# Attention, gated convolution and routed experts on one core: raw key projections, a conversion spread over three engines, a mixed order of the last key tiles, six gather buffers and late probabilities

## The chip, the cores and the metric

The kernel runs on one core of a Trainium2 chip. The metric is the device time in microseconds. Three runs of the kernel before gave 601.50, 601.49 and 603.31 us, a median of 601.5.

## The reference

Three stages are fused. What is computed, cut to its core:

```python
# 1. linear attention; q, k, v are (4, 8, 576, 64), w_phi is (64, 128)
proj = einsum('bhsd,df->bhsf', x, w_phi)
proj = proj - max(abs(proj), axis=-1)
phi  = concat([exp(proj), exp(-proj)])            # 256 features
kv, z = phi(k)^T v, sum_s phi(k)                  # per batch and head
x = phi(q) kv / (phi(q) z + 1e-6)                 # (4, 576, 512)
# 2. gated causal convolution, 5 taps per channel
gate = sigmoid(sum_k conv_w[k] * x[s - 4 + k])
y = (gate * (x @ w_val)) @ w_out
# 3. routing and experts, 8 experts, hidden size 1024
logits = y @ w_gate
e = argmax(logits) at s == 0 or where sigmoid(y @ w_local) < 0.5, else the token's before
p = exp(logits - max); p /= sum(p) + 1e-9
out = p[e] * (relu(y @ w1[e]) @ w2[e])
```

All arrays are float32; w_val, conv_w and w_out are handed to the chip as float64 words.

## The kernel before, in words

The 4 x 576 tokens are 18 tiles of 128. Most products run in a faster single-pass format (fp32r): an operand is split into a high part (a cast on ScalarE, `hi_of`, L48) and a low part (the difference, `lo_of`, L51), and three products take the place of one float32 product: high by high, high by low, low by high.

**Keys, about 4 to 91 us.** For each tile a DMA brings `raw`, `split` (L104) makes `qkh` on ScalarE and `qkl` on GpSimd, and `proj` (L114) multiplies it by `w_phi`, which stands twice on a block diagonal, so that one product serves two heads. A call of `proj` makes half a tile (four heads): two head pairs by three products. Only key tile 0 skips the split: it multiplies `raw` by `wraw` in float32, one product for each head pair (L123). VectorE takes the maximum `m` (L131) and subtracts it, `pp` (L133); ScalarE forms both exponentials `ex`; TensorE adds `kv` (L158). Between these, VectorE converts w_val, w_out and conv_w from float64 words (`from64`, L299 to L323): eight chunks of 128 x 512, six VectorE steps each, of which L319 masks an exponent, L320 and L321 scale and add; four of the chunks' low parts per matrix are GpSimd's.

**Queries and mixing, about 90 to 282 us.** Query tiles are projected in the same way; `tq` (L181) transposes, `nm` (L188) divides, `tx` (L207) transposes x. `conv` (L250) runs taps on VectorE, ScalarE and GpSimd for pairs of tiles. The products of `val` (L379) and `ymm` (L522, the output rows `yps`) are filled in between by a budget in `run` (L602).

**Routing, about 282 to 319 us.** A chain of small steps on VectorE and TensorE builds the tables of gather and scatter columns, `gidx` and `sidx`. The rest of the `yps` products are put between the steps: `yfill(10)` ahead of the first transpose `tp1` (L676, L677), then 5, 5, 5, 5, 3 and all that remain. Then 30 products into `idle` (L757 to L759) use TensorE until the first rows have been gathered. They read `ohl`, whose buffer is let go afterwards.

**Experts, about 319 to 590 us.** Ten static units: eight experts of two row tiles and two overflow units of three row tiles. For each unit, GpSimd gathers the rows `xg` from `y_d` (L812, three buffers, L811), `rows` (L816) transposes and splits them and reads the probabilities `p` (L828 to L835) on VectorE, `unit` (L839) does the first layer `hp` (L850), the activations `hh` on ScalarE and `hlo` on VectorE (L852, L853), the second layer `op` (L862) and the scatter `out` (L868). The next unit's gather is issued as a unit starts (L899); its `rows` are called in `mid` after the unit's first output tile (L911). `between` converts the next unit's weights, `w1h`, `w2h` on ScalarE and `w1l`, `w2l` on VectorE.

The program's order on each engine is the scheduler's: it places the instructions by a model of their times within what data and buffers allow, except where `pin` (L410) keeps an order or `issue_after` holds one instruction behind another. Each engine then works strictly in its order.

Of the kernel before, what the change touches and what calls it, by code (L numbers as in the profile page):

```python
# [30 lines left out]
YLAG = 4  # L31
WARM = 30
FRESH = -1.5 * 2.0 ** -23


@with_exitstack
def body(ctx, tc, qT, kT, v1, wbd, w_val, conv_w, w_out, w_gl, w1, w2, out):
# [66 lines left out]
    def split(nm, t):  # L104

        if t >= NT or (nm, t) in hl_t or (nm, t) == ("k", 0):
            return
        hi = ap.tile([128, 4, 128], F32R, tag="qkh", name="qkh", bufs=2)
        lo = ap.tile([128, 4, 128], F32R, tag="qkl", name="qkl", bufs=2)
        hi_of(A, hi, raw_t[nm, t])  # L110
        lo_of(G, lo, raw_t[nm, t], hi)
        hl_t[nm, t] = (hi, lo)

    def proj(nm, t, hh):  # L114
        raw = raw_t[nm, t]
        if nm == "k" and hh == 1:
            pj = ps_b.tile([128, 4, 128], F32, tag="b", name="pj")
        else:
            pj = ps_p.tile([128, 4, 128], F32, tag="pj", name="pj")
# [55 lines left out]
    def xcols(g):  # L175
        return [(off, n, s == 0, off + 4 * (i + 1)) for i, (off, n, b, s) in enumerate(segments(g * 256, 256))]

    def pq(t, hh):
        pq_t[t, hh] = proj("q", t, hh)

    def tq(t, hh):  # L181
        pp = pq_t.pop((t, hh))
        tp = ps_a.tile([128, 4, 128], F32, tag="a", name="tp")
        for h in range(4):
            PE.transpose(tp[:, h, :], pp[:, h, :], ident)  # L185
        qp_t[t, hh] = both_exp(tp)

    def nm(t, hh):  # L188
        qp = qp_t.pop((t, hh))
        if hh == 0:  # L190
            x_t[t] = ap.tile([128, H, DH], F32, tag="x", name="x", bufs=2)
        ps = ps_a.tile([128, 4, VW], F32, tag="a", name="num")
        for h in range(4):
# [105 lines left out]
    def from64(raw, n, tag):  # L299
# [11 lines left out]

        def first():
            V.tensor_scalar(f, hi, 0x07ffffff, 3, op0=ALU.bitwise_and, op1=ALU.logical_shift_left)
            A.activation(af, hi.bitcast(F32), AF.Abs)

        return f, [
            first,
            lambda: V.scalar_tensor_tensor(b, hi, -0x40000000, f, ALU.bitwise_and, ALU.bitwise_or),
            lambda: V.tensor_scalar(m, b, -0x800000, None, op0=ALU.bitwise_and),  # L319
            lambda: V.scalar_tensor_tensor(mf, top, 0.5, mf, ALU.add, ALU.mult),  # L320
            lambda: V.scalar_tensor_tensor(ff, mf, 2.0 ** -36, bf, ALU.mult, ALU.add),  # L321
            lambda: V.scalar_tensor_tensor(ff, af, 2.0 ** -15, ff, ALU.is_ge, ALU.mult),
        ]  # L323

# [252 lines left out]

    order = []
    for kind in ("k", "q"):
        order += [(kind, t) for t in range(NT)]  # L580
    items = [(kind, t, hh) for kind, t in order for hh in range(2)]
# [60 lines left out]
    route_consts()  # L642
    run(lambda i: (0, 0) if i < 0 else ((i + 1) * 13 // 10 - i * 13 // 10, 0) if i < 36 else (5, 2), lambda i: 2.2 if i > 38 else 0)
    attx.close()
# [30 lines left out]
    tp = pst([NT, 128], "tp1")  # L675
    yfill(10)  # L676
    pin(PE.transpose(tp, rc["code"], ident))  # L677
# [130 lines left out]
    def gather(gcols):  # L808
        xs = []
        for gc in gcols:  # L810
            xg = fx.tile([128, YW], F32, tag="xg", name="xg", bufs=3)  # L811
            G.indirect_dma_start(out=xg, out_offset=None, in_=y_d, in_offset=bass.IndirectOffsetOnAxis(ap=gc, axis=0))  # L812
            xs.append(xg)
        return xs

    def rows(xs, probs):  # L816
# [4 lines left out]
        for j, xg in enumerate(xs):  # L821
# [5 lines left out]
            lo_of(V, xl[:, :, sl], xp, xh[:, :, sl])  # L827
            p = fx.tile([128, 1], F32, tag="p", name="p", bufs=6)  # L828
            if isinstance(probs, int):
                V.tensor_copy(p, xg[:, D + probs:D + probs + 1])  # L830
            else:
                es = fx.tile([128, E], F32, tag="es", name="es")
                V.tensor_scalar(es, io8, probs, None, op0=ALU.is_equal)
                V.tensor_tensor(es, es, xg[:, D:YW], ALU.mult)
                V.tensor_reduce(p, es, axis=AX.X, op=ALU.add)  # L835
            pv.append(p)
        return xh, xl, pv

    def unit(hl, x, scols, between, mid):  # L839
# [5 lines left out]
        for f in range(8):  # L845
# [6 lines left out]
            A.activation(hh[:, f, 0:n], hp[:, 0:n], AF.Relu)  # L852
            V.scalar_tensor_tensor(hlo[:, f, 0:n], hp[:, 0:n], 0.0, hh[:, f, 0:n].bitcast(F32), ALU.max, ALU.subtract)  # L853
            if f % 2 == 1:
                between()
        for j in range(len(pv)):
            op = ps_f.tile([128, 512], F32, tag="op", name="op", bufs=2)
# [33 lines left out]
    xs = gather(cols(gidx, units[0][0], units[0][1]))  # L891
    cur_x = rows(xs, unit_probs(0))
    for i, (c0, n, e) in enumerate(units):
        last = i + 1 == len(units)
        nxt = {}
        work = []
        if not last:
            nxt["w"], pieces = unit_weights(i + 1)
            nxt["xs"] = gather(cols(gidx, units[i + 1][0], units[i + 1][1]))  # L899
            started = [p() for p in pieces[:3]]  # L900
            todo = pieces[3:]
# [7 lines left out]
        def mid():  # L909
            if not last:  # L910
                nxt["x"] = rows(nxt["xs"], unit_probs(i + 1))  # L911

# [49 lines left out]
```

## Time and profile before

| what | value |
|---|---|
| median of three runs | 601.5 us |
| profiled execution | 600.88 us, its span 599.2 us |
| TensorE (PE) | 565.9 us busy, 94% of the span |
| VectorE (DVE) | 373.3 us, 62% |
| ScalarE (ACT) | 314.3 us, 52% |
| GpSimd (POOL) | 231.4 us, 39% |

The profile is of one execution, which took 600.88 us: 1.7 us of it lie outside the span. Line numbers are those of the kernel before. "PEld" is the weight load of TensorE, which overlaps its products. In rows of instructions, a group in square brackets is the time that the engine stood idle before it, and what ended that. The matmul records overlap by design, so a product's price in a full stretch is the distance between starts, not the length of a record.

### The profile page before, as it was taken

Reading aid. Unit: us, or ns where it says so; the run is one execution under the profiler, and the core shown is the slowest. Engines: PE = TensorE matmul, PEld = TensorE weight load, DVE = VectorE, ACT = ScalarE, POOL = GpSimd, SP = SyncE. Lnnn points to the kernel's source line nnn. Section 1 sums busy time; section 2 is a strip of 40 time slices with the busy share of each in tenths; the row PEclk is TensorE's granted clock in tenths of the full one; section 3 lists DMA queues with packets and bytes.
Section 4 is the critical chain, followed back from the end, with each engine's and each line's share of the span. In section 5 each row is a group of like instructions: output and inputs, shape, how many; then the busy total and the mean of one; then the engine's idle time right before and its main releaser. Section 6 shows DMA issues by size and latency. Waiting matters only on the chain. (4 is left out here: it accounts for less than half of the span.)

```text
span 599.2 us, 13671 instructions
## 1 busy us (share of the span) xinstructions
PE 565.9 (94%) x5545; PEld 497.4 (83%) x5546; DVE 373.3 (62%) x744; ACT 314.3 (52%) x581; POOL 231.4 (39%) x257
## 2 busy tenths in 40 slices
PE   7997998999999999998998999999998989999993
PEld 6886987889888988886775888988987879898982
DVE  6999859688877877478504766666554746460110
ACT  5767855665766655555215565564553646441210
POOL 4454323489878876472204102302302123011001
PEclk9999999999999999999998999999999999999997
DMA  8933422101110001034226877866866648520000
GB/s 278 339 101 124 131 74 59 49 2 37 36 38 2 21 19 38 19 124 139 111 107 200 288 237 254 268 181 189 284 186 203 203 137 276 179 90 35 18 18 35
DMA packets 46017, 76.82 MB, mean 128 GB/s; under 512 B 3839, under 2 KB 22399, under 8 KB 45952
## 3 DMA queue, kind: packets, MB, share of 16 engines
q1 hardware_dynamic: 39840, 60.55, 32.5%
q0 software_dynamic: 3520, 10.58, 4.9%
q10 hardware_dynamic: 2592, 4.79, 2.1%
q8 instruction: 45, 0.74, 0.5%
q14 instruction: 20, 0.16, 0.1%
HBM read 66.39 MB, written 10.56 MB: 128 GB/s over the span
## 5 line engine op out<-in xcount | busy, mean ns | idle before, releaser
L868 POOL DMA_INDIRECT out<-osb,sidx x22 | 28.6, 1302 | 206.7 <-ACT osb L867 161.4
L850 PE MATMUL hp<-xh,w1h 128*128 128x256 f32 (+1 forms) x320 | 94.6, 296 | 7.3 <-DVE hlo L853 5.8
L850 PE MATMUL hp<-xh,w1l 128*128 128x256 f32 (+1 forms) x320 | 94.2, 294 | 0.0
L850 PE MATMUL hp<-xl,w1h 128*128 128x256 f32 (+1 forms) x320 | 93.8, 294 | 0.0
L850 PEld LDWEIGHTS hp<-xh,w1h 128*128 128x128 f32 x320 | 60.8, 190 | 10.4 <-DVE hlo L853 7.1
L862 PE MATMUL op<-w2h,hh 128*128 128x512 f32 x176 | 69.1, 401 | 0.2 <-ACT hh L852 0.2
L51 DVE TENSOR_TENSOR w2l<-wraw,w2h 128x1024 fp32r<-128x1024 f32 x40 | 48.9, 1224 | 32.1 <-ACT w2h L48 22.4
L51 POOL TENSOR_TENSOR qkl<-raw,qkh 128x512 fp32r<-128x512 f32 x35 | 46.7, 1334 | 55.5 <-ACT qkh L48 55.4
L862 PE MATMUL op<-w2l,hh 128*128 128x512 f32 x176 | 67.9, 395 | 0.0
L862 PE MATMUL op<-w2h,hlo 128*128 128x512 f32 x176 | 66.8, 395 | 0.0
L51 DVE TENSOR_TENSOR w1l<-wraw,w1h 128x1024 fp32r<-128x1024 f32 x40 | 48.9, 1250 | 22.6 <-ACT w1h L48 22.6
L131 DVE TENSOR_REDUCE m<-pj 128x4 f32<-128x512 f32 x72 | 49.1, 685 | 22.0 <-PE pj L128 21.9
L265 DVE SCALAR_TENSOR_TENSOR acc<-xT,tfs,acc 128x256 f32<-128x256 f32 (+1 forms) x112 | 53.9, 486 | 13.3 <-ACT acc L263 12.0
L850 PEld LDWEIGHTS hp<-xh,w1l 128*128 128x128 f32 x320 | 60.7, 190 | 1.5
L850 PEld LDWEIGHTS hp<-xl,w1h 128*128 128x128 f32 x320 | 60.5, 189 | 0.0
L48 ACT CAST w2h<-wraw 128x1024 fp32r<-128x1024 f32 x40 | 41.8, 1049 | 34.0 <-DMA wraw<-w 25.2
L853 DVE SCALAR_TENSOR_TENSOR hlo<-hp,hh 128x256 fp32r<-128x256 f32 (+1 forms) x80 | 33.9, 445 | 39.6 <-ACT hh L852 39.5
L852 ACT ACTIVATE hh<-hp 128x256 fp32r<-128x256 f32 (+1 forms) x80 | 31.2, 404 | 48.0 <-PE hp L850 47.6
L48 ACT CAST w1h<-wraw 128x1024 fp32r<-128x1024 f32 x40 | 40.4, 1052 | 29.6 <-DMA wraw<-w 29.6
L133 DVE TENSOR_TENSOR pp<-pj,m 128x512 f32<-128x512 f32 x72 | 48.8, 683 | 2.5 <-PE tp L185 0.8
L158 PE MATMUL kv<-v,ex 128*64 128x65 f32 (+1 forms) x1280 | 46.9, 224 | 3.3 <-DVE kvsb L170 1.4
L158 PEld LDWEIGHTS kv<-v,ex 128*64 128x64 f32 (+1 forms) x1280 | 41.0, 137 | 9.3 <-DVE kvsb L170 1.7
(192 smaller groups left out, 1364.5 us busy)
## 6 DMA issues: line engine op xcount, KB each, us to landing
wraw<-w SPq DMA_DIRECT2D x80, 512.0 KB, 4.5
v<-v SPq DMA_DIRECT2D x18, 260.0 KB, 3.2
y_d<-ysb ACTq DMA_DIRECT2D x18, 260.0 KB, 2.0
raw<-qT SPq DMA_DIRECT2D x18, 256.0 KB, 3.4
raw<-kT SPq DMA_DIRECT2D x17, 256.0 KB, 5.0
wr<-w_val SPq DMA_DIRECT2D x4, 512.0 KB, 7.4
wr<-w_out SPq DMA_DIRECT2D x4, 512.0 KB, 7.6
xg<-y_d,gidx POOLq DMA_INDIRECT x22, 5.4
```

Source lines behind the costliest of these rows:

```text
L48: (A.copy if eng is A else eng.tensor_copy)(hi, src)
L51: eng.tensor_tensor(lo, src, hi.bitcast(F32), ALU.subtract)
L131: V.tensor_reduce(m, pj, axis=AX.X, op=ALU.max, apply_absolute_value=True)
L133: V.tensor_tensor(pp, pj, m.unsqueeze(2).to_broadcast([128, 4, 128]), ALU.subtract)
L158: PE.matmul(kv_ps[b][blk // 7][mh * 64:mh * 64 + 64, (blk % 7) * VW:(blk % 7 + 1) * VW], lhsT=kp_t[t, hh][off:off + n, sg, h, mh * 64:mh * ...
L265: W["tap"] = V.scalar_tensor_tensor(acc[c], xs, cw[:, kk, c:c + 1], acc[c], ALU.mult, ALU.add)
L850: PE.matmul(hp[:, 0:n], lhsT=wt[:, k, f * 128:(f + 1) * 128], rhs=xt[:, k, 0:n], start=(i == 0), stop=(i == 11))
L852: A.activation(hh[:, f, 0:n], hp[:, 0:n], AF.Relu)
L853: V.scalar_tensor_tensor(hlo[:, f, 0:n], hp[:, 0:n], 0.0, hh[:, f, 0:n].bitcast(F32), ALU.max, ALU.subtract)
L862: PE.matmul(op, lhsT=ht[:, f, sl], rhs=wt[:, f, :], start=(i == 0), stop=(i == 23))
L868: G.indirect_dma_start(out=out, out_offset=bass.IndirectOffsetOnAxis(ap=scols[j], axis=0), in_=osb, in_offset=None, bounds_check=T - 1, oo ...
```

## The change

`split` returns for every key tile, so all 18 key tiles are projected in float32 from `raw`. `from64` has four steps instead of six: VectorE keeps L313, L318, L319 and L322, ScalarE makes the scaled top word, and GpSimd does the product and the sum. The last three key tiles (MIX = 3) alternate with the first three query tiles; query tiles 0 to 3 take their two PSUM tiles from `ps_b`. `yfill(10)` is `yfill(18)`. The gathers have six buffers (XG = 6), the rows of unit 1 are gathered right behind those of unit 0, and those of unit i + 2 in `mid` of unit i. The probabilities are computed in `unit`, issued behind the last `hlo` of that unit.

```diff
     def split(nm, t):
-        if t >= NT or (nm, t) in hl_t or (nm, t) == ("k", 0):
+        if t >= NT or (nm, t) in hl_t or nm == "k":
             return
...
-        if nm == "k" and hh == 1:
+        if nm == "k" and hh == 1 and t < NT - MIX:
             pj = ps_b.tile([128, 4, 128], F32, tag="b", name="pj")
...
+    def early(t):
+        return ps_b if t <= MIX else ps_a
...
-        tp = ps_a.tile([128, 4, 128], F32, tag="a", name="tp")
+        tp = early(t).tile([128, 4, 128], F32, tag="ab"[early(t) is ps_b], name="tp")
...
-            lambda: V.scalar_tensor_tensor(mf, top, 0.5, mf, ALU.add, ALU.mult),
-            lambda: V.scalar_tensor_tensor(ff, mf, 2.0 ** -36, bf, ALU.mult, ALU.add),
+        def join():
+            V.scalar_tensor_tensor(b, hi, -0x40000000, f, ALU.bitwise_and, ALU.bitwise_or)
+            A.activation(ff, top, AF.Copy, bias=2.0 ** -37, scale=2.0 ** -36)
+        def low():
+            V.tensor_scalar(m, b, -0x800000, None, op0=ALU.bitwise_and)
+            G.tensor_tensor(mf, ff, mf, ALU.mult)
+            G.tensor_tensor(ff, mf, bf, ALU.add)
...
-    for kind in ("k", "q"):
-        order += [(kind, t) for t in range(NT)]
+    order = [("k", t) for t in range(NT - MIX)]
+    for t in range(MIX):
+        order += [("q", t), ("k", NT - MIX + t)]
+    order += [("q", t) for t in range(MIX, NT)]
...
-    yfill(10)
+    yfill(18)
     pin(PE.transpose(tp, rc["code"], ident))
...
-            xg = fx.tile([128, YW], F32, tag="xg", name="xg", bufs=3)
+            xg = fx.tile([128, YW], F32, tag="xg", name="xg", bufs=XG)
...
+        with tc.issue_after(low.ins):
+            pv = [prob(*z) for z in pv]
...
     cur_x = rows(xs, unit_probs(0))
+    xs = {1: gather(cols(gidx, units[1][0], units[1][1]))}
...
-            nxt["xs"] = gather(cols(gidx, units[i + 1][0], units[i + 1][1]))
...
-                nxt["x"] = rows(nxt["xs"], unit_probs(i + 1))
+                nxt["x"] = rows(xs.pop(i + 1), unit_probs(i + 1))
+                if i + 2 < len(units):
+                    xs[i + 2] = gather(cols(gidx, units[i + 2][0], units[i + 2][1]))
```

**TensorE early in the key stage.** In the kernel before, a half tile is six products of split operands (`qkh`, `qkl` by `wb_hi`, `wb_lo`), between the `kv` products of the half tile before it:

```order
L158 MATMUL kv_221<-v,ex 64x65 x14
L158 MATMUL kv_222<-v,ex 64x65 x2
L128 MATMUL pj<-wb_hi,qkh 128x256
L128 MATMUL pj<-wb_lo,qkh 128x256
L128 MATMUL pj<-wb_hi,qkl 128x256
L128 MATMUL pj<-wb_hi,qkh 128x256
L128 MATMUL pj<-wb_lo,qkh 128x256
L128 MATMUL pj<-wb_hi,qkl 128x256
L158 MATMUL kv_222<-v,ex 64x65 x12
L158 MATMUL kv_223<-v,ex 64x65 x4
```

The same engine in the changed kernel, from its first product on (three key tiles ahead of the first `kv`):

```order
L130 MATMUL pj<-wraw,raw 128x256 x12
L160 MATMUL kv_205<-v,ex 64x65 x14
L160 MATMUL kv_206<-v,ex 64x65 x14
L160 MATMUL kv_207<-v,ex 64x65 x4
L160 MATMUL kv_205<-v,ex 64x65 x14
L160 MATMUL kv_206<-v,ex 64x65 x2
L130 MATMUL pj<-wraw,raw 128x256 x2
L160 MATMUL kv_206<-v,ex 64x65 x12
L160 MATMUL kv_207<-v,ex 64x65 x4
L130 MATMUL pj<-wraw,raw 128x256 x2
```

Two products stand where six stood, each with float32 operands.

**GpSimd in the key stage.** Before, after the constants, it makes the low parts of key tiles and of converted chunks:

```order
L51 TENSOR_TENSOR qkl<-raw,qkh 128x512 x5
L51 TENSOR_TENSOR wval_l<-tfw,wval_h 128x512
L51 TENSOR_TENSOR qkl<-raw,qkh 128x512 x2
L51 TENSOR_TENSOR wval_l<-tfw,wval_h 128x512
L51 TENSOR_TENSOR qkl<-raw,qkh 128x512
L51 TENSOR_TENSOR wval_l<-tfw,wval_h 128x512
```

In the changed kernel the same stretch holds the conversion's product (L328) and sum (L329):

```order
L328 TENSOR_TENSOR tmw<-tfw,tmw 128x512
L329 TENSOR_TENSOR tfw<-tmw,tbw 128x512
L53 TENSOR_TENSOR wval_l<-tfw,wval_h 128x512
L328 TENSOR_TENSOR tmw<-tfw,tmw 128x512
L329 TENSOR_TENSOR tfw<-tmw,tbw 128x512
L53 TENSOR_TENSOR wval_l<-tfw,wval_h 128x512
```

The key tiles' low parts are gone from it, and each chunk has three instructions here instead of one.

**GpSimd's gathers.** Before, with the semaphores that each waits for: three gathers go out together (two for unit 0, one for unit 1), and from the fourth on each waits for a buffer's readers, VectorE and TensorE:

```order
L812 DMA xg<-y_d,gidx 128x520 [waits DMAHW0_49,DMAHW1_49,DVE_49,DMAHW2_49,Activation_49,Pool_49]
L812 DMA xg<-y_d,gidx 128x520 x2
L812 DMA xg<-y_d,gidx 128x520 [waits DMASW0_49,DVE_49,PE_49]
L812 DMA xg<-y_d,gidx 128x520 [waits DMASW1_49,DVE_49,PE_49]
```

In the changed kernel six go out first, and the second of them waits for TensorE:

```order
L822 DMA xg<-y_d,gidx 128x520 [waits DMAHW0_49,DMAHW1_49,DVE_49,DMAHW2_49,Activation_49,Pool_49]
L822 DMA xg<-y_d,gidx 128x520 [waits PE_49]
L822 DMA xg<-y_d,gidx 128x520 x4
L822 DMA xg<-y_d,gidx 128x520 [waits DMASW0_49,DVE_49,PE_49]
```

The instruction on which that `PE_49` counts is the last of the 30 products into `idle`: the second buffer lies where `ohl` lay.

**VectorE in the late units.** Before, the selection of a probability (`es`) that needs the gathered rows of unit 8 stands among the `hlo` of unit 7:

```order
L51 TENSOR_TENSOR w2l<-wraw,w2h 128x1024
L853 SCALAR_TENSOR_TENSOR hlo<-hp,hh 128x256
L834 TENSOR_TENSOR es<-es,xg 128x8 x2
L853 SCALAR_TENSOR_TENSOR hlo<-hp,hh 128x256 x3
L51 TENSOR_TENSOR xl<-xp,xh 128x4x128
L853 SCALAR_TENSOR_TENSOR hlo<-hp,hh 128x256
```

In the changed kernel it stands behind the last `hlo` of unit 8 itself:

```order
L53 TENSOR_TENSOR w2l<-wraw,w2h 128x1024
L53 TENSOR_TENSOR xl<-xp,xh 128x4x128
L867 SCALAR_TENSOR_TENSOR hlo<-hp,hh 128x384 x5
L848 TENSOR_SCALAR es<-io_74,eu_f 128x8 x2
L849 TENSOR_TENSOR es<-es,xg 128x8 x2
L850 TENSOR_REDUCE p<-es 128x1 x2
```

The wait for the gathered rows has left the row of `hlo` instructions.

## Rows read from the trace of the kernel before

**Rows 1.** The page: busy time of each engine, share, instructions.
```profile
PE 565.9 (94%) x5545; PEld 497.4 (83%) x5546; DVE 373.3 (62%) x744; ACT 314.3 (52%) x581; POOL 231.4 (39%) x257
```
**Rows 2.** Stretches: us, busy time and instructions per engine, clock, DMA share, GB/s.
```profile
45.00:60.00 15.00, 11.97 (x201) 10.06 (x201) 15.00 (x25) 11.12 (x21) 6.71 (x5) 1.00 0.39 124
95.00:100.00 5.00, 3.83 (x54) 3.31 (x52) 5.00 (x11) 3.44 (x7) 2.12 (x2) 1.00 0.33 95
100.00:110.00 10.00, 7.61 (x106) 6.59 (x108) 9.87 (x24) 6.14 (x12) 3.24 (x3) 1.00 0.12 34
120.00:130.00 10.00, 9.00 (x121) 8.55 (x120) 8.64 (x23) 6.03 (x13) 9.62 (x12) 1.00 0.01 2
300.00:310.00 10.00, 10.00 (x45) 8.08 (x45) 0.00 (x0) 2.40 (x4) 0.57 (x3) 1.00 0.24 95
```
**Rows 3.** L128 by form, ns min/median/max: the raw products of key tile 0.
```profile
L128 PE MATMUL pj<-wraw,raw x8: 634/634/767, 3.6 to 6.7; 128*128 128x256 f32 x8
```
**Rows 4.** Timeline of TensorE: start us, us; raw products at the start.
```profile
4.61 2.77 PE L128 MATMUL pj<-wraw,raw 128*128 128x256 f32 x6
```
**Rows 5.** Timeline of TensorE: two neighbouring split products at the start, two later.
```profile
7.39 0.42 PE L128 MATMUL pj<-wb_lo,qkh 128*128 128x256 f32 x1
7.61 0.42 PE L128 MATMUL pj<-wb_hi,qkh 128*128 128x256 f32 x1
...
19.59 0.28 PE L128 MATMUL pj<-wb_lo,qkh 128*128 128x256 f32 x1
...
20.06 0.28 PE L128 MATMUL pj<-wb_hi,qkl 128*128 128x256 f32 x1
```
**Rows 6.** VectorE's groups by form: count, busy us, mean ns, idle before.
```profile
L131 DVE TENSOR_REDUCE m<-pj 128x4 f32<-128x512 f32 x72 | 49.1, 685 | 22.0 <-PE pj L128 21.9
L133 DVE TENSOR_TENSOR pp<-pj,m 128x512 f32<-128x512 f32 x72 | 48.8, 683 | 2.5 <-PE tp L185 0.8
L320 DVE SCALAR_TENSOR_TENSOR tmw<-wr,tmw 128x512 f32<-128x512 uint16 x8 | 6.8, 855 | 0.0
L321 DVE SCALAR_TENSOR_TENSOR tfw<-tmw,tbw 128x512 f32<-128x512 f32 x8 | 5.4, 678 | 0.0
```
**Rows 7.** GpSimd's groups by form: the low parts of the tiles.
```profile
L51 POOL TENSOR_TENSOR qkl<-raw,qkh 128x512 fp32r<-128x512 f32 x35 | 46.7, 1334 | 55.5 <-ACT qkh L48 55.4
```
**Rows 8.** VectorE's mask of the exponent, ns min/median/max.
```profile
L319 DVE TENSOR_SCALAR tmw<-tbw x8: 411/418/1486, 15.4 to 108.1; 128x512 int32<-128x512 int32 x8
```
**Rows 9.** Timeline of GpSimd and VectorE at 41.5 us.
```profile
41.53 2.70 POOL L51 TENSOR_TENSOR qkl<-raw,qkh 128x512 fp32r<-128x512 f32 x2
41.61 1.49 DVE L319 TENSOR_SCALAR tmw<-tbw 128x512 int32<-128x512 int32 x1 [0.48 <-POOL wval_l L51]
```
**Rows 10.** Timeline of TensorE: the first step of routing.
```profile
282.33 0.28 PE L677 MATMUL tp<-ident,code 128*18 128x128 f32 x1 [1.69 <-DVE code L520]
```
**Rows 11.** Timeline of TensorE and GpSimd around the first unit's start.
```profile
312.50 6.64 PE L759 MATMUL idle<-ohl,ones 128*128 128x512 bf16 x29
317.19 0.95 POOL L812 DMA_INDIRECT xg<-y_d,gidx  x1 [0.30 <-issue]
320.99 0.66 PE L824 MATMUL xp<-ident,xg 128*128 128x128 f32 x4 [0.92 <-DMA xg<-y_d,gidx]
323.14 0.38 PE L850 MATMUL hp<-xh,w1h 128*128 128x256 f32 x1 [1.50 <-ACT xh L48]
```
**Rows 12.** Timeline of VectorE and TensorE inside the units.
```profile
330.76 0.41 PE L824 MATMUL xp<-ident,xg 128*128 128x128 f32 x2 [0.50 <-DMA xg<-y_d,gidx]
459.98 0.17 DVE L834 TENSOR_TENSOR es<-es,xg 128x8 f32<-128x8 f32 x1 [4.03 <-DMA xg<-y_d,gidx]
461.83 0.39 PE L850 MATMUL hp<-xh,w1h 128*128 128x256 f32 x1 [2.66 <-DVE hlo L853]
488.23 0.38 PE L850 MATMUL hp<-xh,w1h 128*128 128x256 f32 x1 [2.32 <-DVE hlo L853]
```
**Rows 13.** ScalarE's casts of expert weights, and what ended their waits (page).
```profile
L48 ACT CAST w1h<-wraw 128x1024 fp32r<-128x1024 f32 x40 | 40.4, 1052 | 29.6 <-DMA wraw<-w 29.6
```

More of the change, by code (lines that the diff above doesn't have):

```diff
@@ L32 @@
 WARM = 30
+XG = 6
+MIX = 3
 FRESH = -1.5 * 2.0 ** -23
@@ L191, in nm @@
             x_t[t] = ap.tile([128, H, DH], F32, tag="x", name="x", bufs=2)
-        ps = ps_a.tile([128, 4, VW], F32, tag="a", name="num")
+        ps = early(t).tile([128, 4, VW], F32, tag="ab"[early(t) is ps_b], name="num")
         for h in range(4):
@@ L310, in from64, with high @@
         af, bf, mf, ff = [z.bitcast(F32) for z in (a, b, m, f)]
-        def first():
+        def high():
             V.tensor_scalar(f, hi, 0x07ffffff, 3, op0=ALU.bitwise_and, op1=ALU.logical_shift_left)
             A.activation(af, hi.bitcast(F32), AF.Abs)
[L316 to L319, printed above, removed]
-            lambda: V.scalar_tensor_tensor(mf, top, 0.5, mf, ALU.add, ALU.mult),
-            lambda: V.scalar_tensor_tensor(ff, mf, 2.0 ** -36, bf, ALU.mult, ALU.add),
-            lambda: V.scalar_tensor_tensor(ff, af, 2.0 ** -15, ff, ALU.is_ge, ALU.mult),
-        ]
+        def join():
[5 more added lines that the diff above has]
+            G.tensor_tensor(ff, mf, bf, ALU.add)
+        return f, [high, join, low, lambda: V.scalar_tensor_tensor(ff, af, 2.0 ** -15, ff, ALU.is_ge, ALU.mult)]
     def setup_small():
@@ L576, in fill @@
             st["credit"] -= c
-    order = []
-    for kind in ("k", "q"):
-        order += [(kind, t) for t in range(NT)]
+    order = [("k", t) for t in range(NT - MIX)]
+    for t in range(MIX):
+        order += [("q", t), ("k", NT - MIX + t)]
+    order += [("q", t) for t in range(MIX, NT)]
     items = [(kind, t, hh) for kind, t in order for hh in range(2)]
@@ L642, in body @@
     route_consts()
-    run(lambda i: (0, 0) if i < 0 else ((i + 1) * 13 // 10 - i * 13 // 10, 0) if i < 36 else (5, 2), lambda i: 2.2 if i > 38 else 0)
+    i0 = 2 * (NT - MIX)
+    run(lambda i: (0, 0) if i < 0 else ((i + 1) * 13 // 10 - i * 13 // 10, 0) if i < i0 else (5, 2), lambda i: 2.2 if i > i0 + 2 else 0)
     attx.close()
@@ L827, in rows, with prob @@
             lo_of(V, xl[:, :, sl], xp, xh[:, :, sl])
[L828 to L836, printed above, removed]
-        return xh, xl, pv
+            pv.append((xg, probs))
+        return xh, xl, pv
+    def prob(xg, probs):
+        p = fx.tile([128, 1], F32, tag="p", name="p", bufs=6)
+        if isinstance(probs, int):
+            V.tensor_copy(p, xg[:, D + probs:D + probs + 1])
+        else:
+            es = fx.tile([128, E], F32, tag="es", name="es")
+            V.tensor_scalar(es, io8, probs, None, op0=ALU.is_equal)
+            V.tensor_tensor(es, es, xg[:, D:YW], ALU.mult)
+            V.tensor_reduce(p, es, axis=AX.X, op=ALU.add)
+        return p
     def unit(hl, x, scols, between, mid):
@@ L852, in unit @@
             A.activation(hh[:, f, 0:n], hp[:, 0:n], AF.Relu)
-            V.scalar_tensor_tensor(hlo[:, f, 0:n], hp[:, 0:n], 0.0, hh[:, f, 0:n].bitcast(F32), ALU.max, ALU.subtract)
+            low = V.scalar_tensor_tensor(hlo[:, f, 0:n], hp[:, 0:n], 0.0, hh[:, f, 0:n].bitcast(F32), ALU.max, ALU.subtract)
             if f % 2 == 1:
                 between()
+        with tc.issue_after(low.ins):
+            pv = [prob(*z) for z in pv]
         for j in range(len(pv)):
```

## Prediction

> **What bounds the kernel now.** I read the page first. TensorE is busy in 565.9 of 599.2 us [rows 1], so the whole kernel leaves 33 us to be won by removing waits, and anything that makes TensorE's own work longer is paid in full wherever it is busy. Then I cut the span into stretches, to see which waits are inside those 33 us. At 45 to 60 us TensorE is busy for 11.97 of 15 us, and VectorE for all 15.00: here VectorE bounds, and TensorE loses 3.03 us. At 95 to 100 and 100 to 110 us, where the queries begin, TensorE loses 1.17 and 2.39 us beside a VectorE that is busy for 5.00 of 5 and 9.87 of 10; at 120 to 130 it loses 1.00 with GpSimd at 9.62 of 10 [rows 2]. Late in the routing, at 300 to 310 us, TensorE is full and VectorE has nothing. So the limits differ by stage: VectorE in two stretches of the first 130 us, TensorE nearly everywhere else. Last I read TensorE's timeline for single waits with one releaser: 1.69 us before the first step of routing [rows 10], the start of unit 0 [rows 11], and three waits in the expert units that go back to gathered rows [rows 12].
>
> **The change part by part.** Durations come from the profiled execution of 600.88 us, and the sum is made against it. The median of the runs is 601.5, so 0.6 us is added at the end.
>
> *Raw key projections (cost, A).* For 17 tiles, four head-pair products each take the place of 12: 68 raw products replace 204 split ones. The raw product is in the trace only at the very start. Six of its records take 2.77 us [rows 4], and the last runs 0.634 us [rows 3]: (2.77 - 0.634) / 5 = 0.427 us from record to record. Key tile 0 has four products and eight records [rows 3], so a product is two records, 0.854 us. That is a price at the slow start: there the distance between split products is 7.61 - 7.39 = 0.22 us, later it is (20.06 - 19.59) / 4 = 0.1175 us [rows 5]. The engine was at the lower of its two levels (1.2 GHz) then and at the upper (2.4 GHz) later. No row shows a raw product at the upper level, so I bound it. Above: it stays at 0.854, and A is 68 x (0.854 - 3 x 0.1175) = 68 x 0.5015 = +34.1 us. Below: it halves with the level to 0.427, and A is 68 x 0.0745 = +5.1 us. Scaled as the split product scaled (0.22 / 0.1175 = 1.87), it is 0.457 and A is +7.1 us. I take the halving, since in the slow rows the raw record (0.427) and the split step (0.22) stand in the ratio 1.94, which leaves little that would not scale; about 0.5 us comes on top for a tile that is still projected at the slow step, where a raw product costs 0.854 - 0.66 = 0.19 more, for two to three products. A = +5.6 us. It is on the path where TensorE is full; in the VectorE-bound stretch part of it fills TensorE's idle time, which I count in the next term.
>
> *Conversion on three engines (gain, B).* VectorE loses L320 and L321, 0.855 + 0.678 = 1.53 us a chunk [rows 6], 12.3 us over eight chunks; ScalarE gets one more activation a chunk, in a stage where it is busy for 11.12 of 15 us [rows 2]. GpSimd gets two tensor operations a chunk, which I price at its low parts, 1.334 us [rows 7], 21.3 us in all, and loses the key tiles' low parts (17 x 1.334 = 22.7 us), so it carries no more than before. What is added is a wait: VectorE's last step of a chunk now needs GpSimd's two, 2.67 us after the mask. Behind it in VectorE's order stand the next `m` and `pp` of a key tile, for which the exponentials and then TensorE's `kv` wait. If one `m` and one `pp` (0.685 + 0.683 = 1.37) stand between mask and last step, about 1.3 us of wait is left in a chunk, near the 1.53 saved; with more between, nothing is left. So the ends are -3.03 (all idle time of that stretch goes) and, should the wait be open in every chunk and lengthened, a loss that I price as a rival. I take -2.3, three quarters of the idle time, because removing the splits also removes GpSimd's `qkl` from in front of the conversion's own work.
>
> *Mixed order (gain, C).* TensorE's idle time at the start of the queries is 1.17 + 2.39 + 1.00 = 4.56 us [rows 2]. Key work (`kv`, raw products) now lies beside the first three query tiles, whose VectorE work is long; yet VectorE's work is the same in total, only spread, and the first stretch of queries alone that follows still has convolution taps beside it. The ends are -4.56 and +2.4 (a second stretch like the one at 100 to 110 us appears behind the mixing). I take -2.6, a little over half of what there is.
>
> *yfill(18) (gain, D).* The first transpose of routing waits 1.69 us for `code` [rows 10]. Eight more `yps` products stand ahead of it; at 300 to 310 us 45 of them fill 10.00 us [rows 2], 0.222 each, 1.78 us in all: just the wait. They are work that is moved, not added. What is left to cover the later steps is shorter by 1.78 us, but the products go on until the tables are done and the table step at 311.85 follows them directly, so no cover is gone. The ends are -1.69 and 0 (a later step loses what this one gains). D = -1.7 us.
>
> *Six buffers (cost, E).* The second gather now waits for the last of the `idle` products, which ends at 312.50 + 6.64 = 319.14 us; before, it was issued at 317.19 [rows 11]. It lands, as before, 320.99 - 317.19 = 3.80 us after its issue, so the second `xp` starts at 322.95. Before, the first `hp` followed it by 323.14 - 320.99 = 2.15 us, of which 0.66 are the transposes and 1.50 the wait for two casts; the first tile's cast will then be done, so half of that wait counts: 322.95 + 0.66 + 0.75 = 324.4 us. Ends: 0 (the wait is hidden) and 322.95 + 2.15 - 323.14 = +2.0. E = +1.2 us.
>
> *Probabilities and early gathers (gain, F).* In the static units VectorE stands at `es` for 4.03 us for gathered rows, with the `hlo` of the unit queued behind it, and TensorE then waits 2.66 us for `hlo`; the same happens at 488.23 with 2.32, and at 330.76 TensorE itself waits 0.50 for gathered rows [rows 12]. With the rows gathered a unit earlier and `es` behind the last `hlo`, all three go: 2.66 + 2.32 + 0.50 = 5.5 us. What could be late next is `p` for the scaling of the output; it is wanted after 24 second-layer products, and costs VectorE three small steps, so I count nothing. Ends: -5.5 and 0.
>
> Sum: +5.6 - 2.3 - 2.6 - 1.7 + 1.2 - 5.5 = -5.3 us. 600.88 - 5.3 + 0.6 = **596.2 us**.
>
> **The rivals.**
>
> *All stalls go (592.3 us).* B takes all 3.03, C all 4.56, and the second gather's wait is hidden: 0.7 + 2.0 + 1.2 = 3.9 us less. For it: VectorE's work falls by 12 us in just the stages where it bounds. Against: in both stretches VectorE is full, not nearly full, so a smaller load need not bring it below TensorE.
>
> *The expert units give nothing back (601.7 us).* F = 0. ScalarE waited 29.6 us in all for the expert weights that it casts [rows 13]; if these transfers set the pace, the 2.66 and 2.32 us reappear at a later cast and `w1l`. For it: that sum. Against: the two waits of TensorE named a releaser that stood behind gathered rows, and in the rest of the units TensorE hardly waits.
>
> *The conversion stays with GpSimd (about 603 us).* In the trace a VectorE mask that takes 0.418 us in the median took 1.49 us beside GpSimd's low parts [rows 8, 9]. If GpSimd's two new steps and VectorE's operations hold each other up, each pair takes 2.67 + 2 x 0.68 = 4.03 us, VectorE waits 4.03 - 1.37 = 2.66 us, and after the 1.53 saved it has lost 1.13 us a chunk. Over the four chunks that I put in bounded stretches this is +4.5 in place of -2.3: 596.2 + 6.8 = 603.0. Against: GpSimd had 15 - 6.71 us free at 45 to 60 us [rows 2]. The Trainium skill states such a rule (page "SBUF — State Buffer", section "Who interferes with whom"): a VectorE instruction with two SBUF inputs, or in a two-port mode, and a GpSimd instruction that reads SBUF share one read interface, and whichever comes second is blocked for the other's whole length. By that rule this rival is the case; the trace agrees in the one row at 41.61, and shows no GpSimd pair beside VectorE for the new steps.
>
> *Slower: the raw product is dearer than half.* Its place is TensorE's own path in the first 90 us, its price 68 times what it takes above 0.427. The gain of 5.3 us is used up at 0.427 + 5.3 / 68 = 0.505 us a product, and at 0.53 the kernel is slower by over 0.3%. At 0.854 it ends at 596.2 + 29.0 = 625 us. For it: the only rows of a raw product [rows 3, 4]. Against: the split products of the same stretch sped up by 1.87 [rows 5].
>
> **How the numbers follow.** Chances: the forecast 0.55 (its own range 593 to 599), all stalls go 0.10, units give nothing back 0.13, the conversion stays with GpSimd 0.12, the raw product is dearer 0.10. 0.3% of 601.5 is 1.8 us, about what a measurement of this kernel can tell from no change, so "same" is 599.7 to 603.3. Faster: 0.55 + 0.10 = 0.65. Same: 0.13 and half of the third rival, 0.06: 0.19. Slower: 0.10 + 0.06 = 0.16. The range of 591.0 to 602.5 holds the forecast, the first two rivals and nearly half of the third, some 0.83.
>
> **What would show it.** A: distances between raw records at 20 to 90 us, 0.214 expected each (two a product); a distance near 0.43 means the last rival. B: VectorE under 15.00 in the stretch at 45 to 60 us and short waits before the last step of a chunk; long ones with GpSimd as releaser mean the third rival. C: TensorE's idle time at the start of the queries down from 4.56 to about 2. D: no wait over 0.3 us before the first transpose of routing. E: the second gather issued just after the last `idle` product, the first `hp` about 1 us later after the tables than before. F: no `es` between `hlo` rows, and no TensorE wait over 1 us in the units; waits with the casts of weights as releaser mean the second rival. The prediction is wrong if TensorE's busy time grows by more than 8 us, or if the key stage ends later than before by more than 3 us.

## The result, and the profile after

The changed kernel took 606.82 us in the median of 20 runs, the kernel before 603.36 us in 20 runs (the first three of which gave the 601.5 shown above). The ratio is 1.0064, with a 95% interval of 1.0042 to 1.0087: by the ratio slower by 3.9 us, where 596.2 us was forecast, and outside the range. The profiled execution took 603.33 us, with a span of 601.5; it was the fastest of the twenty, so its trace shows less of the loss than the median.

The page after, the busy times and the clock in 40 slices of 15 us (a digit is the granted clock in tenths):

```profile
PE 571.5 (95%) x5477; PEld 498.0 (83%) x5478; DVE 363.0 (60%) x726; ACT 311.1 (52%) x573; POOL 238.9 (40%) x258
...
PEclk9999997899999999999999899999999999999997
```

TensorE is 5.6 us busier than in [rows 1], VectorE 10.3 us less. What is new is the clock in slices 7 and 8, 90 to 120 us. Stretches of the changed kernel (us, busy time and instructions of PE, PEld, DVE, ACT, POOL, then the granted clock, DMA share, GB/s):

```profile
45.00:60.00 15.00, 14.11 (x228) 10.83 (x228) 12.16 (x21) 11.02 (x22) 3.83 (x3) 1.00 0.44 122
...
94.00:96.00 2.00, 0.33 (x3) 0.12 (x1) 0.69 (x1) 0.62 (x1) 2.00 (x2) 1.00 0.00 0
96.00:98.00 2.00, 0.00 (x0) 0.00 (x0) 0.55 (x1) 0.00 (x0) 1.42 (x2) 0.77 0.23 62
98.00:110.00 12.00, 11.80 (x52) 11.20 (x52) 1.53 (x3) 4.90 (x13) 1.27 (x1) 0.50 0.05 13
```

The first row answers to [rows 2]: in the stretch where VectorE was full, it is now busy for 12.16 us and TensorE for 14.11 instead of 11.97. The other three are a hole: TensorE does nothing from 94.3 to 98.2 us, its clock falls to 0.50 (1.2 of 2.4 GHz), and it stays there for some 12 us more, in which TensorE never stops. TensorE's timeline through the hole (start us, us, instruction, count, idle time before and its releaser):

```profile
94.04 0.28 PE L130 MATMUL pj<-wb_hi,qkl 128*128 128x256 f32 x1
98.20 1.12 PE L369 MATMUL tps<-ident,tfw 128*128 128x128 f32 x4 [3.88 <-DVE tfw L331]
99.11 6.83 PE L377 MATMUL wps<-wgl,woT 128*128 128x9 f32 x32
105.80 1.09 PE L191 MATMUL tp<-ident,pp 128*128 128x128 f32 x4
...
110.23 1.49 PE L203 MATMUL num<-kvsb,ex 128*64 128x65 f32 x36
```

`tps` are the four transposes of the eighth converted chunk, the last of w_out; `wps` are the folds, products of 9 columns (counted here in records, eight for each of the four chunks of w_out). The wait is for the chunk's last step on VectorE. That step waits for GpSimd, whose two conversion steps have the low part of a query tile (`qkl`) between them. VectorE, then GpSimd, in the same stretch:

```profile
94.36 0.69 DVE L133 TENSOR_REDUCE m<-pj 128x4 f32<-128x512 f32 x1 [0.81 <-PE pj L130]
97.45 0.69 DVE L331 SCALAR_TENSOR_TENSOR tfw<-taw,tfw 128x512 f32<-128x512 f32 x1 [2.40 <-POOL tfw L329]
```

```profile
93.70 1.28 POOL L328 TENSOR_TENSOR tmw<-tfw,tmw 128x512 f32<-128x512 f32 x1 [1.09 <-DVE tmw L327]
94.94 1.26 POOL L53 TENSOR_TENSOR qkl<-raw,qkh 128x512 fp32r<-128x512 f32 x1
96.16 1.26 POOL L329 TENSOR_TENSOR tfw<-tmw,tbw 128x512 f32<-128x512 f32 x1
```

In routing, the first transpose follows the `yps` products without a wait, where [rows 10] had 1.69 us (timeline of TensorE):

```profile
292.47 0.39 PE L540 MATMUL yps<-wout_h,gl 128*128 128x512 f32 x1
292.70 0.27 PE L687 MATMUL tp<-ident,code 128*18 128x128 f32 x1
```

It stands at 292.70 instead of 282.33. The first of the `yps` products ahead of it, in the kernel before and in the changed one:

```profile
278.05 0.51 PE L532 MATMUL yps<-wout_h,gh 128*128 128x512 f32 x1
```

```profile
288.41 0.50 PE L540 MATMUL yps<-wout_h,gh 128*128 128x512 f32 x1
```

It too is 10.4 us later, so the stages before routing lost 10.4 us; the eight products moved ahead of the transpose lie where its wait was. From there to the first idle product routing takes 32.6 us, where it took 34.5. Unit 0, as in [rows 11] (TensorE, and one row of GpSimd):

```profile
321.03 6.64 PE L769 MATMUL idle<-ohl,ones 128*128 128x512 bf16 x29
331.25 0.66 PE L834 MATMUL xp<-ident,xg 128*128 128x128 f32 x4 [2.00 <-DMA xg<-y_d,gidx]
332.58 0.58 PE L864 MATMUL hp<-xh,w1h 128*128 128x256 f32 x1 [0.68 <-ACT xh L50]
```

```profile
327.95 0.95 POOL L822 DMA_INDIRECT xg<-y_d,gidx  x1 [1.81 <-PE idle L769]
```

The second gather does wait for the last idle product, and from the first idle product to the first `hp` it takes 332.58 - 321.03 = 11.55 us, where it took 10.64. From that `hp` to the start of the last output product it then takes 259.1 us (332.6 to 591.7), where it took 266.2 (323.1 to 589.3). The page's group for the first product of a hidden block shows it, idle time and releaser last: in the kernel before, and in the changed one.

```profile
L850 PE MATMUL hp<-xh,w1h 128*128 128x256 f32 (+1 forms) x320 | 94.6, 296 | 7.3 <-DVE hlo L853 5.8
```

```profile
L864 PE MATMUL hp<-xh,w1h 128*128 128x256 f32 (+1 forms) x320 | 94.3, 295 | 2.4 <-DVE hlo L867 1.7
```

So the expert part gained 7.1 us, routing gained 1.8, unit 0 starts 0.9 later, and the stages before routing lost 10.4: together 2.4 us, about the difference of the spans (2.3). The hole lies in the part that lost.

### The profile page after: what moved, and what is told of

It reads as the page before. It is cut to its first block, busy times and chain, and to the rows that moved or that the text cites. A ratio compares the mean times of both kernels' runs of the same rounds, so it can differ in the third digit from the quotient of the medians.

```text
span 601.5 us, 13514 instructions
## 1 busy us (share of the span) xinstructions
PE 571.5 (95%) x5477; PEld 498.0 (83%) x5478; DVE 363.0 (60%) x726; ACT 311.1 (52%) x573; POOL 238.9 (40%) x258
## 5 line engine op out<-in xcount | busy, mean ns | idle before, releaser
L864 PE MATMUL hp<-xh,w1h 128*128 128x256 f32 (+1 forms) x320 | 94.3, 295 | 2.4 <-DVE hlo L867 1.7
L884 POOL DMA_INDIRECT out<-osb,sidx x22 | 30.4, 1381 | 117.3 <-ACT osb L883 72.6
L822 POOL DMA_INDIRECT xg<-y_d,gidx x22 | 35.8, 1625 | 95.4 <-DVE p L845 73.1
L53 DVE TENSOR_TENSOR w1l<-wraw,w1h 128x1024 fp32r<-128x1024 f32 x40 | 47.6, 1223 | 25.9 <-ACT w1h L50 25.6
L135 DVE TENSOR_TENSOR pp<-pj,m 128x512 f32<-128x512 f32 x72 | 49.4, 686 | 12.8 <-PE tp L191 10.4
```

The costliest lines, as they stand in the source:

```text
L53: eng.tensor_tensor(lo, src, hi.bitcast(F32), ALU.subtract)
L135: V.tensor_tensor(pp, pj, m.unsqueeze(2).to_broadcast([128, 4, 128]), ALU.subtract)
L864: PE.matmul(hp[:, 0:n], lhsT=wt[:, k, f * 128:(f + 1) * 128], rhs=xt[:, k, 0:n], start=(i == 0), stop=(i == 11))
L884: G.indirect_dma_start(out=out, out_offset=bass.IndirectOffsetOnAxis(ap=scols[j], axis=0), in_=osb, in_offset=None, bounds_check=T - 1, oo ...
```

## The experiments

There were two theories at first. H: the hole is made by GpSimd's pair of steps in the conversion. R: there is no special hole, the raw products are dearer than forecast. A third, M, later called O: the mixed order makes the hole. All ratios are to the kernel before, and numbers in brackets behind them are 95% intervals.

**e1: the last chunk on VectorE.** Only the eighth chunk keeps the old steps.

```diff
-            r, ops = from64(rr, 512, "w")
+            r, ops = from64(rr, 512, "w", nm_ == "out" and c == 3)
```

> The changed kernel, but the eighth converted chunk (the last of w_out) keeps the old six steps on VectorE; the other seven go over GpSimd as changed. TensorE's order up to this chunk's transposes is the same. Theory H (a hole): the loss against the kernel before is the wait of TensorE for this chunk (3.88 us idle at 94 to 98 us, VectorE's last step behind GpSimd's pair with a query tile's low part between its two halves) and the half clock that follows it until about 110 us, together some 8 us; it expects no idle time over 1.5 us there, the granted clock at 1.00 from 90 to 130 us, and a time 8 us below the changed kernel's, a ratio to the kernel before of about 0.993. Rival R (raw products): the loss is the 68 float32 products of the keys, which cost more than the 5.6 us forecast; it expects the ratio to stay at 1.006, within 0.002. Rival M (mixed order): the hole comes from the three query tiles among the keys and opens again elsewhere before 130 us, with the clock down again; ratio 1.003 to 1.007.

Measured: 603.21 us, 1.0019 (0.9994 to 1.0043). TensorE and VectorE at the hole:

```profile
97.83 0.66 PE L378 MATMUL tps<-ident,tfw 128*128 128x128 f32 x4 [3.21 <-DVE tfw L338]
98.32 6.61 PE L386 MATMUL wps<-wgl,woT 128*128 128x9 f32 x32
```

```profile
94.66 0.69 DVE L133 TENSOR_REDUCE m<-pj 128x4 f32<-128x512 f32 x1
95.27 1.78 DVE L337 SCALAR_TENSOR_TENSOR tfw<-tmw,tbw 128x512 f32<-128x512 f32 x1
97.08 0.69 DVE L338 SCALAR_TENSOR_TENSOR tfw<-taw,tfw 128x512 f32<-128x512 f32 x1
```

The hole stays, with 3.21 us instead of 3.88, though no step of this chunk's conversion is on GpSimd any more. H falls in this form: the ratio lies above its 0.993 and just below what M gave. One step of 0.69 us now took 1.78: it ran while GpSimd made a low part (95.24 to 96.51 us).

**e2: the last chunk's transposes later.** The conversion is as changed; only the program's place of `tps` and the fold of the last chunk moves (the comments are not in the kernel).

```diff
+        if (nm, t, hh) == ("q", 2, 1):        # in proj, after its products
+            for f in held:
+                f(mm)
...
+                    if c == 3:
+                        held.append(tail)      # tail: the four transposes, woT, the fold
+                    else:
+                        tail()
```

> The changed kernel, but the four transposes of the last w_out chunk (and its fold) are issued later, behind the second half of the projection of query tile 2; the conversion itself is as changed, with GpSimd's pair in it. Theory H says that the wait costs because it stands alone in TensorE's row: with the transposes later, TensorE has the other queries' transposes and the next raw products in front of it, so the gap is below 2 us and the clock stays at 1.00; ratio to the kernel before about 0.993 to 0.997. If instead VectorE's own wait for GpSimd (2.4 us) holds back the next maximum and difference, TensorE's gap only changes its releaser, the clock falls as before, and the ratio stays at 1.004 to 1.007. Rival R expects 1.006.

Measured: 591.60 us, 0.9837 (0.9797 to 0.9877), 2.3% below the changed kernel and faster than any of the three ranges. VectorE's last step of the chunk, and TensorE's transposes of it:

```profile
97.49 0.68 DVE L335 SCALAR_TENSOR_TENSOR tfw<-taw,tfw 128x512 f32<-128x512 f32 x1
```

```profile
102.79 1.13 PE L131 MATMUL pj<-wraw,raw 128*128 128x256 f32 x4
...
104.82 0.66 PE L382 MATMUL tps<-ident,tfw 128*128 128x128 f32 x4
```

The chunk is done at the same time as in the changed kernel (97.49 against 97.45), but now nothing on TensorE waits for it: the transposes, projections and `num` of the queries stand in front. So the lateness of the chunk is not the cost; its place in TensorE's row is. The first routing transpose is at 281.7 us, 11.0 sooner. Against what was expected, the clock still falls once here, without a gap, behind 24 folds:

```profile
90.00:95.00 5.00, 5.00 (x59) 4.63 (x58) 3.68 (x7) 3.04 (x7) 2.42 (x2) 1.00 0.32 94
95.00:100.00 5.00, 5.00 (x31) 4.66 (x32) 1.98 (x3) 3.30 (x8) 1.39 (x2) 0.66 0.01 3
100.00:105.00 5.00, 5.00 (x84) 4.24 (x84) 3.77 (x8) 3.13 (x6) 3.74 (x3) 1.00 0.19 53
```

**e3: five gather buffers.** `XG = 5`.

> The changed kernel with five gather buffers instead of six. The second gather then no longer waits for the last idle product. Theory: the first product of unit 0 comes about 1 us sooner after the last table step than in the changed kernel, and no gather of a later unit is late for it; 1 us less, a ratio to the kernel before of about 1.005. Rival: the gathers one buffer shorter come late for the two overflow units and give up to 2 us back; ratio 1.006 to 1.009.

Measured: 609.68 us, 1.0132 (1.0094 to 1.0170), above both ranges. The first `hp` comes 10.6 us after the first idle product, the 1 us sooner that was expected, but from it to the last output product it takes 267.4 us instead of 259.1. The longest wait is in unit 1 (ScalarE, then TensorE):

```profile
362.62 1.04 ACT L50 CAST w1h<-wraw 128x1024 fp32r<-128x1024 f32 x1 [3.47 <-DMA wraw<-w]
...
364.85 1.04 ACT L50 CAST w2h<-wraw 128x1024 fp32r<-128x1024 f32 x1
365.80 0.38 ACT L866 ACTIVATE hh<-hp 128x256 fp32r<-128x256 f32 x1
```

```profile
366.23 0.80 PE L878 MATMUL op<-w2h,hh 128*128 128x512 f32 x1 [3.47 <-ACT hh L866]
```

ScalarE stands 3.47 us at a cast of weights that have not landed, with `hh` queued behind it, and TensorE stands for `hh`. That is the mechanism of the prediction's second rival, in one place; in the changed kernel TensorE waits 1.55 us at the same place. Around it the granted clock falls as well, to 0.52 in the mean from 365 to 372 us. The rival of this run, late gathers for the overflow units, does not show: behind 367 us TensorE waits nowhere for over 0.5 us. Why the weights are later with five buffers stays open.

**e4: the expert part alone**, put into the kernel before (buffers, early gathers, late probabilities).

> The kernel before with only the expert part of the change: six gather buffers, rows gathered a unit earlier, probabilities behind the last hlo of their unit. Keys, conversion, order and routing are as before. Theory: from the first product of unit 0 to the last output product it takes 259 us instead of 266 (the changed kernel's own difference), less 1 us for the second gather's wait: 6 us faster, ratio 0.990. Rival: part of the 7 us comes from the clock or from the schedule of the changed kernel and not from this part; ratio 0.993 to 1.000.

Measured: 595.14 us, 0.9887 (0.9847 to 0.9927), 6.8 us faster, as expected.

**e5: keys before queries.** `MIX = 0`. With the order, `MIX` also sets which PSUM tiles the last keys and the first queries take, and from which half tile on `run` takes up the conversion faster (number 30 with 3, 36 with 0), so these change too.

> The changed kernel with MIX = 0: all key tiles stand before all query tiles again; raw keys, the conversion on three engines, yfill(18) and the expert part are as changed. Theory O (order): the hole at 94 to 110 us is made by TensorE's row, in which the mixed order puts the last chunk's transposes where nothing else is ready, and goes with the mixed order: no idle time over 1.5 us and a clock of 1.00 around the last chunk, a ratio to the kernel before of 0.985 to 0.993. Theory H (GpSimd's pair in the conversion makes it): the hole stays near the last chunk, ratio 1.000 to 1.007.

Measured: 594.99 us, 0.9867 (0.9835 to 0.9900). TensorE at the last chunk:

```profile
102.02 0.60 PE L191 MATMUL tp<-ident,pp 128*128 128x128 f32 x4
103.07 0.66 PE L369 MATMUL tps<-ident,tfw 128*128 128x128 f32 x4 [0.45 <-DVE tfw L331]
...
107.39 2.85 PE L377 MATMUL wps<-wgl,woT 128*128 128x9 f32 x24
```

The same conversion, with GpSimd's pair, costs TensorE 0.45 us here. Theory O holds: the mixed order, with what hangs on `MIX`, is worth 1.0064 against 0.9867, 2.0% or 11.9 us; e2 keeps all of it and moves only the last chunk's transposes and fold. At full clock 24 folds take 2.8 us, 0.12 each, where the changed kernel's 32 took 6.7, 0.21 each.

**e6: the conversion on VectorE** for all chunks, mixed order kept.

```diff
-        return f, [high, join, low, ...]
+        return f, [first, ...]                # the six steps of the kernel before
...
-    run(... (i + 1) * 13 // 10 - i * 13 // 10 ...)
+    run(... (i + 1) * 18 // 10 - i * 18 // 10 ...)
```

> The changed kernel with the conversion of the kernel before for all chunks (six steps on VectorE), taken up at a rate of 1.8 steps for each half tile instead of 1.3, so that it still ends before the queries need it. Theory O: TensorE's row at the last chunk is the same and the hole stays (idle over 2.5 us, half clock until about 108 us); VectorE has 12 us more to do in the first 90 us, and TensorE waits for it there; ratio 1.004 to 1.015. Theory H: without GpSimd's pair the hole closes; ratio 0.990 to 0.998.

Measured: 603.97 us, 1.0019 (0.9996 to 1.0041), below what O gave and above what H gave. TensorE's waits and the clock:

```profile
96.10 0.36 PE L130 MATMUL pj<-wb_hi,qkh 128*128 128x256 f32 x1 [2.03 <-DVE pp L135]
99.57 1.12 PE L367 MATMUL tps<-ident,tfw 128*128 128x128 f32 x4 [2.52 <-DVE tfw L328]
```

```profile
100.00:105.00 5.00, 5.00 (x26) 5.00 (x25) 0.00 (x0) 1.02 (x4) 1.26 (x1) 0.50 0.18 52
```

The hole is there without any GpSimd step in the conversion. So the pair is one way to be late, and a full VectorE (busy for 5.00 of 5 us at 90 to 95 us) another.

**e7: raw keys alone**, in the kernel before.

```diff
-        if t >= NT or (nm, t) in hl_t or (nm, t) == ("k", 0):
+        if t >= NT or (nm, t) in hl_t or nm == "k":
```

> The kernel before with only the split of the key tiles left out, so that all key tiles are projected in float32. Theory: a half tile's raw block is 1.06 us where the split block was 0.90 us (both from traces), 34 half tiles make 5.4 us; GpSimd and ScalarE lose the split's work, which returns up to 2 us; ratio 1.005 to 1.009. Rival R: raw products cost over 8 us; ratio over 1.013. A ratio under 1.002 would say that the waits for split operands were worth as much as the dearer products.

Measured: 609.74 us, 1.0121 (1.0085 to 1.0157), 7.3 us, between the two. In its trace 4.3 us are there at the first routing transpose (286.61 against 282.33), though the clock also fell once on the way, for 3.4 us at 105 us, which it did not in the profile of the kernel before; the rest is in the units, where TensorE stands 3.5 us for `hh` at 363 us.

**e8: later transposes, and idle products that don't read `ohl`** (66 of 256 columns in place of 30 of 512).

```diff
-        pin(PE.matmul(idle, lhsT=rc["ones"], rhs=ohl[:, 0:4, :]...))
+        pin(PE.matmul(idle[:, 0:256], lhsT=ident.bitcast(BF16)[:, 0:128], rhs=ident.bitcast(BF16), ...))
```

> The changed kernel with the last chunk's transposes later, and the idle products reading the identity matrix instead of the table's one-hot rows (66 products of 256 columns in place of 30 of 512), so that the second gather waits for the table product and not for the last idle one. Theory: the first unit's first product comes 1 to 2 us sooner after the table than with the transposes later alone (11.7 us from the first idle product to it), 9.5 to 10.7 us; ratio to the kernel before 0.980 to 0.983. Rival: the start of the units is paced by the weights and by the clock that falls in the wait, and what the gather gives is lost there; ratio 0.984 or more.

Measured: 592.96 us, 0.9824 (0.9789 to 0.9858), not distinguishable from e2. The second gather went out right behind the first, at 316.56 us, yet the first `hp` came 13.7 us after the first idle product, later than in e2 (11.65): the first rows landed late.

```profile
321.06 0.66 PE L851 MATMUL xp<-ident,xg 128*128 128x128 f32 x4 [3.21 <-DMA xg<-y_d,gidx]
```

The ratio lies in the theory's range, but not for the theory's reason: the units did not start sooner. In e3, where the second gather did not wait either, they did (10.6 us). So without the wait the start can be 0.9 us sooner or 2 us later, and why the first rows landed late in e8 (their transposes begin 6.6 us behind the gather's issue, in e2 3.8) stays open.

**e9, e10, e11: the split of the keys put back**, in e2, in e5 and in the changed kernel. The edit is e7's, reversed.

> The kernel with the last chunk's transposes later (ratio 0.984 to the kernel before), and with the split of the key tiles put back, so that only key tile 0 is raw. Theory: the raw block of a half tile costs 0.16 us more than the split one, so the split gives 5.4 us back, less what VectorE and GpSimd then lose to each other (17 low parts of 1.3 us return to GpSimd beside the conversion's pairs, up to 3 us of waits): ratio 0.975 to 0.981. Rival: with the conversion's pairs, GpSimd's row of low parts is what the keys wait for, and raw keys pay for themselves: 0.984 or more.

> The changed kernel without its raw keys and without its mixed order: left of the change are the conversion on three engines, yfill(18) and the expert part. Theory: no hole (0.987 with raw keys), and 5.4 us less for the split products less up to 3 us of waits: ratio 0.978 to 0.984. Rival: GpSimd's pairs behind 17 low parts make VectorE and TensorE wait in the key stage, ratio 0.987 or more.

> The changed kernel with only the split of the key tiles put back; the mixed order stays, and TensorE's row around the last chunk's transposes is of the same form (the six products of a query's half tile, the four transposes, 16 folds). Theory O: the hole is the order's and not the raw products', so it stays (an idle time over 2 us before these transposes, the clock at 0.50 behind it): ratio 0.994 to 1.002, that is 1.006 less 5.4 us and up to 3 us of waits more. Rival R: without raw products the loss goes: ratio 0.990 or less with the clock at 1.00.

Measured: e9 0.9828 (0.9790 to 0.9866) beside e2's 0.9837; e10 0.9884 (0.9848 to 0.9921) beside e5's 0.9867; e11 1.0029 (1.0003 to 1.0054) beside the changed kernel's 1.0064. e9 lies between its theory and its rival, e10 on the rival's side, e11 just above what the theory gave. Beside the conversion on three engines the raw keys cost between -1 and 2 us, and none of the three differences is clear of the intervals. And e11's hole is the same without them:

```profile
99.23 1.11 PE L369 MATMUL tps<-ident,tfw 128*128 128x128 f32 x4 [3.94 <-DVE tfw L331]
```

R falls too: the hole is made neither by the raw products nor by GpSimd's pair, but by the mixed order, through the place that it gives the last chunk's transposes. The fastest versions are e2, e8 and e9, 589 to 595 us in all runs, 1.6 to 1.8% faster than the kernel before.

## Why the prediction was wrong, point by point

**The step that failed is C, the mixed order.** It was put at -2.6 us with ends of -4.56 and +2.4; e5 against the changed kernel measures +11.9 us. The working took the idle time that was there before and asked how much of it would go. It did not ask which instruction would stand first in TensorE's row when the last chunk is late. The upper end was one more stretch of waits at the full clock. In fact there is one wait, 3.88 us, which is of that size, and behind it TensorE works at half clock for 12 us: the 32 folds take 6.7 instead of 3.8 us (0.12 each in e5), the three groups of four transposes 0.87 instead of 0.49 us each, four raw records 1.84 instead of 1.06, which with the first transposes (0.91 instead of 0.49) makes about 5.2 us more. Wait and clock together are 9.1 us; the trace of e5 is 8.5 us sooner than that of the changed kernel at the first `yps` ahead of routing (279.88 us), that of e2 11.0. How the two would be split if the clock had not fallen was not tried in a run of its own. An estimate for all runs: the mean granted clock of the whole span was 0.968 to 0.982 in the twenty runs of the changed kernel and 0.985 to 0.990 in the six of e5, in the mean 0.9758 and 0.9865. The difference, 0.0107 of some 605 us, is 6.5 us, over half of the 11.9, wherever in the span the clock fell.

The sign that the prediction named for C shows little of this. TensorE's idle time in its three stretches fell from 4.56 to 3.20 us (about 2 was expected), all of it in the row below; the rest of the loss stands in the clock, 0.71 here and 0.50 in the next 10 us.

```profile
95.00:100.00 5.00, 1.80 (x9) 1.80 (x10) 0.75 (x2) 0.62 (x1) 3.54 (x3) 0.71 0.18 52
```

**A, raw keys: the price of a product was right, its effect on the time was not.** The distance between raw records is now 0.216 us, half of the 0.427 of the start [rows 4]. A half tile's block, from its first product to the next `kv`, in the changed kernel and in the kernel before:

```profile
60.85 1.13 PE L130 MATMUL pj<-wraw,raw 128*128 128x256 f32 x4
61.91 0.28 PE L160 MATMUL kv<-v,ex 128*64 128x65 f32 x2
```

```profile
19.37 0.39 PE L128 MATMUL pj<-wb_hi,qkh 128*128 128x256 f32 x1
...
20.27 0.45 PE L158 MATMUL kv<-v,ex 128*64 128x65 f32 x7
```

1.06 against 0.90 us; 34 half tiles make 5.4 us, with 5.6 forecast. The rival of a dearer product is out. (One sum of it is off: at 0.53 us a product, 68 x 0.103 = 7.0 us leave 1.7 us of loss, 0.28% and not over 0.3%.) But the term is not one number. Alone in the kernel before, raw keys cost 7.3 us (e7); beside the conversion on three engines they cost nothing that is clear of noise (e9 to e11). The sum added A and B as if each had its price by itself. A likely reason is GpSimd, which makes the low parts of the split keys and, in the changed kernel, the conversion's two steps; no run singles it out.

**B, the conversion: the size in its stretch was right, its worth by itself was not shown.** TensorE's idle time in the stretch at 45 to 60 us fell from 3.03 to 0.89 us, a gain of 2.1 with 2.3 forecast, with the raw products and the lighter VectorE together. With the keys split, the conversion and yfill(18) add nothing that the runs can show: e10 has 0.9884 and e4, without both, 0.9887, each good to some 2 us, where B and D were to give 4.0 us. The wait that was added, by form:

```profile
L331 DVE SCALAR_TENSOR_TENSOR tfw<-taw,tfw 128x512 f32<-128x512 f32 x8 | 5.5, 692 | 7.4 <-POOL tfw L329 7.4
```

7.4 us in eight chunks, 0.93 each, where 1.3 was worked out. The third rival named this wait and its place, but not what it did: e6 has the hole without it. Its rule of the shared read interface (the Trainium skill, "SBUF — State Buffer", "Who interferes with whom") shows again in e1, 1.78 us for a step of 0.69 beside a low part on GpSimd.

**D, yfill: right.** The 1.69 us are gone, no later step of routing waits over 0.3 us, and routing is 1.8 us shorter.

**E, six buffers: +0.9 us at the first `hp`, with +1.2 forecast**, by the wait that was named. Taking that wait away brought the time back in e3 and not in e8.

**F, probabilities and gathers: right, and too small.** With E it was -4.3 us; e4 measures -6.8. TensorE's idle time before `hp` fell from 7.3 to 2.4 us. The second rival appears in single places: waits of 1.55 us for `hh` at 364.35 us and of 1.68 for `hlo` at 374.7, and more in e3 and e7.

Without the mixed order the change gives 0.9867, 8.0 us, against 2.7 us forecast for the terms without C. So the other terms together came out better than forecast, and one term, with its sign wrong, took all of it and 3.9 us more.

## What to carry to other kernels

Where a change alters the order of work, look up on the bounding engine which instruction stands first whenever a late operand is due, and what is queued behind it: an operand ready at 98 us cost nothing in e2 and 9 us or more in the changed kernel. Price a lone wait on TensorE as the wait plus the work at half clock that may follow it: here 3.88 us became 9.1. Look at the clock as well as at idle time. And do not take the terms of two edits as independent: raw keys cost 7.3 us alone and nothing clear of noise beside the new conversion. A side chain that is always late belongs behind work that is ready, not at the place where a model of times has it just in time.

## What the runs showed of the hardware

- In the changed kernel the granted clock stayed at 0.50 for 12 us in which TensorE was busy for 11.80 of 12.00 us, most of it folds of 9 columns and transposes. It also fell without any gap just before: in e2 behind 24 folds (0.66 in the stretch from 95 to 100 us), and in e5 at 111 us behind 24 of them. In the kernel before, two groups of 16 folds between 112.8 and 117.8 us passed at 1.00. No run changes the folds alone, so what part they have in it is not shown.
- The clock once fell behind waits of under 1 us each: in e2 it was 0.61 at 34 to 36 us, behind two waits of 0.61 and 0.76 us for `kvsb`, which the changed kernel's profile has too, without the fall.
